# One store per 128 output rows in chunks 0 to 6 of an attention and feed-forward kernel

## The chip, the cores and the metric

The kernel runs on one core of a Trainium2 chip. The metric is the device time of one execution in microseconds (us). Before the change the median of three runs is 240.99 us (240.96 to 241.0). One execution was recorded by the hardware profiler; it took 240.52 us, of which the profile's span covers 238.4 us.

## What is computed

Eight batches of linear attention (8 heads, 576 tokens, 64 columns per head) are followed by a feed-forward block over all 4608 tokens. All inputs and the output are float32; the kernel computes its products in 16-bit floats.

```python
q_s = np.exp(q - np.max(q, axis=-1, keepdims=True))
q_s = q_s / (np.sum(q_s, axis=-1, keepdims=True) + 1e-09)
k_s = np.exp(k - np.max(k, axis=2, keepdims=True))
k_s = k_s / (np.sum(k_s, axis=2, keepdims=True) + 1e-09)
kv = np.einsum('bhsd,bhse->bhde', k_s, v)
y = np.einsum('bhsd,bhde->bhse', q_s, kv)
# feed-forward over x = y as [4608, 512]
a = x @ w1 ; b = x @ w2           # [4608, 1024] each
h = (a * b) @ w3                  # [4608, 1024]
out = h @ w_out                   # [4608, 512]
```

The softmax of q runs along the 64 columns, that of k along the tokens (axis 2). The kernel folds w3 and w_out into one matrix W3O of 1024 x 512 once, so that each token goes through w1, w2 and W3O only.

## The kernel before

**Tiling.** The 576 tokens of a batch are seen as 64 groups of 9 (`"(p j) c"`, p = 64, j = 9). A chunk is a set of 512 tokens: chunks 0 to 7 take tokens j = 0 to 7 of one batch each, chunk 8 takes the tokens j = 8 of all eight batches. Each chunk runs through `up` (matmuls with w2, then w1, line 779), `bs` (a cast of the w2 product from PSUM), `ab` (their product, line 794), and then four `down` steps of 128 tokens each (line 801), each with an eviction `os` (line 806, through the helper `copy` of line 323) into a buffer `osb` of 128 partitions x 512 float32, and a store `st` (line 824). A row block tb of chunk c covers j = 2 tb in partitions 0 to 63 and j = 2 tb + 1 in partitions 64 to 127. `osb` has four buffers, used in the order of the evictions; an eviction into a buffer waits until the store of what it held has landed.

**Order.** `ORDER` (line 77) lists every step by name, and each engine executes its own steps in that order: `st.4.2` is the store of row block 2 of chunk 4, `down.6.0` the down product of row block 0 of chunk 6, `xm.7.0` a product of attention that makes the x tile of chunk 7, and so on. A step that waits holds up everything behind it on its engine.

**SP.** SP (SyncE) issues four sorts of transfers in this order: the two loads of q for batch 0 (512 and 640 KB); the seventeen `LATE` loads of q, k and v for batches 2 to 7 (1152 KB each; line 402); twelve transposing transfers `qd` (line 637) that turn the normalised exponentials of q (tile `en`) into `qT` for batches 2 to 7, which `xm` needs; and the stores. In chunks 0 to 7 a store step issues two transfers of 64 rows each (line 827), in chunk 8 one transfer per row block of 128 rows, the last block in two halves of the columns (line 809). That makes 2 + 17 + 12 + 64 + 5 = 100 transfers on SP. They signal eight semaphores in turn, the first transfer the first one.

**End.** After its last transfer SP waits at the end of the program (line 915) for all eight semaphores, one after the other, and then meets the other engines at a barrier.

**The last part of attention.** The last two transposing transfers are `qd.7.0` and `qd.7.1`. On SP the stores `st.4.1`, `st.4.0` and `st.3.3` stand before the former, `st.5.1` and `st.4.2` between the two, and `st.4.3`, `st.5.2` and `st.5.0` behind the latter. With those of the earlier chunks, 20 row blocks of stores stand ahead of `qd.7.1`, and 8 of chunks 4 to 6 behind it. `xm.7.0`, `xm.7.1` and `xt.7` on TensorE wait for `qd.7.1`, and all of chunk 7 waits for them.

Of the kernel before, what the change touches and what calls it, by code (L numbers as in the profile page):

```python
# [229 lines left out]
def kernel(  # L230
# [11 lines left out]
    nc = tc.nc  # L242
    B, H, S, D = q.shape
# [7 lines left out]
    HALF = P // G  # L251
    HH = H // G
    NHP = HH // 2
    NJ = S // HALF
# [33 lines left out]
    st = {}  # L288
# [24 lines left out]
    TREE = [b < TREES for b in range(B)]  # L313
    VCAST = [b < VCASTS for b in range(B)]
    DMATP = []
    XMS = 3
    DMAT = [[b > DMATS or (b, p) in DMATP for p in range(2)] for b in range(B)]
    SPLIT = [0, 1]
# [153 lines left out]
    def attention(b):  # L472
# [176 lines left out]
        def XRING(name):  # L649
            if name[1] < XMS:  # L650
                return "att"
            return "pab" if name[0] == "xt" else "po" if name[2] else "att"
# [112 lines left out]
    def chunk(c):  # L765
# [54 lines left out]
        def os2(tb, c0, c1, eng):  # L820
            st["osb", c, tb, c0] = work.tile([P, c1 - c0], F32, tag="osb", name="osb", bufs=4)
            copy(eng, st["osb", c, tb, c0], st["po", c, tb, c0][:, 0:c1 - c0])

        def store(tb):
            for i in range(2):
                b, j = c, 2 * tb + i
                nc.sync.dma_start(
                    out=out[b * S:(b + 1) * S, :].rearrange("(p j) c -> p j c", j=NJ)[:, j, :],
                    in_=st["osb", c, tb][i * HALF:(i + 1) * HALF, :])

        A = plan.add
        nf = len(SUBS[c])
# [19 lines left out]
        for sub in range(nf):  # L852
            for tb in range(4):
                if not SUBS[c][sub][0] <= tb * P < SUBS[c][sub][1]:
                    continue
                first = tb * P == SUBS[c][sub][0]
                needs = (([("ab", c, sub, u) for u in range(nu - 1)] + [("W3O", ft) for ft in range(N_FT)]
                          if first else []) + ([("down", c, tb - 1)] if tb else []))
                late = [("ab", c, sub, nu - 1)] if first else []
                if c < B:  # L860
                    A(("down", c, tb), "PE", 1.75, lambda tb=tb: down(tb), needs, takes="po", after=late)
                    A(("os", c, tb), moves(C), 0, lambda eng, tb=tb: os(tb, eng), [("down", c, tb)],
                      lead=EVICT, gives=[("down", c, tb)], takes="osb")
                    A(("st", c, tb), "SP", 1.15, lambda tb=tb: store(tb), [("os", c, tb)], lead=1e3,
                      gives=[("os", c, tb)], size=P * C * 4)
                    continue
                cuts = [0, C // 2, C] if tb == 3 else [0, C]
                for c0, c1 in zip(cuts, cuts[1:]):
                    it = (c, tb, c0) if c1 < C else (c, tb)
                    A(("down", *it), "PE", 0.02 + 1.73 * (c1 - c0) / C,  # L870
                      lambda tb=tb, c0=c0, c1=c1: down2(tb, c0, c1), needs, takes="po", after=late)
                    A(("os", *it), moves(c1 - c0), 0,
                      lambda eng, tb=tb, c0=c0, c1=c1: os2(tb, c0, c1, eng), [("down", *it)],
                      lead=EVICT, gives=[("down", *it)], takes="osb")
                    A(("st", *it), "SP", 0.57, lambda tb=tb, c0=c0, c1=c1: tail(tb, c0, c1),
                      [("os", *it)], lead=1e3, gives=[("os", *it)], size=P * (c1 - c0) * 4)
                    needs, late = needs + [("down", *it)], []
# [42 lines left out]
```

## Time and profile before

| | |
|---|---|
| median of three runs | 240.99 us (240.96 to 241.0) |
| the profiled execution, its own time | 240.52 us |
| its span in the profile | 238.4 us |
| bytes written to HBM | 9.44 MB, all of it the output |
| bytes read from HBM | 38.80 MB |
| stores of chunks 0 to 7 | 64 transfers of 128 KB |
| stores of chunk 8 | 3 transfers of 256 KB, 2 of 128 KB |

The page of the profile gives each engine's busy time; the span cut into 40 equal slices with the busy share of each engine and of the 16 DMA engines; the DMA queues; the chain of work that ended last, followed back from the end; and the costliest groups of instructions. Times are in us from the start of the span. PE is TensorE's matmul, PEld its weight load, DVE is VectorE, ACT ScalarE, POOL GpSimd, SP SyncE; SPq is SP's own queue, which issues transfers. A DMA packet is one contiguous piece that one DMA engine moves. "q1 hardware_dynamic" are the transfers that SP issued; "q0 software_dynamic" those that GpSimd issued, all in the first 58 us. The share of a queue is the time that its packets took, as a share of 16 engines over the stretch asked for; packets overlap a little, so it can pass 100%.

### The profile page before, as it was taken

How to read it: one execution, taken by the hardware profiler on the slowest of the kernel's cores; microseconds unless marked ns; L12 is line 12 of the kernel's file. 1: busy time of each engine (PE TensorE's matmuls, PEld its weight loads, DVE VectorE, ACT ScalarE, POOL GpSimd, SP SyncE). 2: the span in 40 equal slices, each digit the busy share in tenths (PEclk: the TensorE clock that was granted, in tenths of full speed). 3: DMA queues.
4: the chain of work that ended last, by engine and by line, in shares of the span. 5: the costliest groups of instructions: out<-in, count | busy, mean ns of one | idle time of the engine just before them, and what ended most of it. 6: DMA issues, size and time to landing. Idle time of an engine off the chain costs nothing.

```text
span 238.4 us, 4957 instructions
## 1 busy us (share of the span) xinstructions
PE 230.7 (97%) x1981; PEld 121.1 (51%) x1981; DVE 180.0 (76%) x275; ACT 120.7 (51%) x221; POOL 112.8 (47%) x74
## 2 busy tenths in 40 slices
PE   7899899999999999999999999999999999999994
PEld 2445559865857544444444444444454444444442
DVE  2977998898899989998998899787567444355610
ACT  1436764668768958768824683557323002200021
POOL 8345445479957986997662933328530000000000
PEclk9999999999999999999999999999999999999999
DMA  6999999999989999688988932540077231030143
GB/s 209 215 294 223 322 220 301 261 370 392 389 210 291 403 205 294 243 235 203 327 270 200 306 147 46 77 111 0 0 150 173 62 71 45 0 91 0 44 132 132
DMA packets 37894, 45.66 MB, mean 192 GB/s; under 512 B 15984, under 2 KB 22384, under 8 KB 37872
## 3 DMA queue, kind: packets, MB, share of 16 engines
q1 hardware_dynamic: 30080, 34.22, 49.3%
q0 software_dynamic: 7792, 11.14, 21.3%
q8 instruction: 15, 0.25, 0.4%
q14 instruction: 7, 0.06, 0.1%
HBM read 38.80 MB, written 9.44 MB: 202 GB/s over the span
## 4 chain that ended last, share of the span: by engine, by line
PE 86%; DMA 5%; DVE 3%; POOL 2%; issue 1%; ACT 1%; POOLq 0%; ACTq 0%
PE pab L779 52%; PE po L801 23%; DMA wosb<-in_moe_w_out_dram 5%; PE po L816 3%; PE pkv L544 2%; PE po L452 2%; PE xm L662 1%; DVE k L519 1%; POOL en L614 1%; POOL w L402 1%; PE po L662 1%; DVE kmx L493 1%; ACT ek L527 0%; PE pkv L554 0%; PE qtp L629 0%
## 5 line engine op out<-in xcount | busy, mean ns | idle before, releaser
L779 PE MATMUL pab<-x,w2sb 128*128 128x512 f16 (+1 forms) x320 | 66.0, 337 | 0.1
L779 PE MATMUL pab<-x,w1sb 128*128 128x512 f16 (+1 forms) x320 | 65.9, 336 | 0.0
L794 DVE TENSOR_TENSOR ab<-pab,bsb 128x512 f16<-128x512 f32 x72 | 48.9, 681 | 16.7 <-PE pab L779 15.2
L801 PE MATMUL po<-W3O,ab 128*128 128x512 f16 x256 | 59.5, 379 | 0.0
L779 PEld LDWEIGHTS <-w1sb 128*128 128x128 f16 x352 | 34.4, 98 | 27.9
L779 PEld LDWEIGHTS <-w2sb 128*128 128x128 f16 x352 | 33.4, 98 | 27.0 <-issue 0.7
L323 ACT CAST bsb<-pab 128x512 f16<-128x512 f32 x49 | 28.3, 585 | 36.5 <-PE pab L779 36.2
L801 PEld LDWEIGHTS <-ab 128*128 128x128 f16 x256 | 24.6, 98 | 28.8 <-issue 0.4
L519 POOL TENSOR_TENSOR k<-k,cb 128x1152 f32<-128x1152 f32 x13 | 33.9, 2626 | 8.1 <-DVE km L496 3.5
L582 POOL TENSOR_TENSOR q<-q,qm 128x1280 f32<-128x1280 f32 (+1 forms) x13 | 27.8, 2142 | 20.7 <-DVE qm L577 12.9
L614 POOL TENSOR_TENSOR en<-eq,qr 128x1024 f16<-128x1024 f16 (+1 forms) x14 | 29.2, 2093 | 17.4 <-DVE qr L607 8.0
L323 ACT COPY osb<-po 128x512 f32<-128x512 f32 (+1 forms) x26 | 14.9, 576 | 35.8 <-PE po L801 28.9
L577 DVE TENSOR_REDUCE qm<-q 128x16 f32<-128x1024 f32 (+1 forms) x16 | 21.4, 1340 | 3.5 <-DMA q<-in_q_dram 3.5
L323 DVE COPY osb<-po 128x512 f32<-128x512 f32 (+1 forms) x11 | 7.3, 667 | 20.8 <-PE po L801 13.7
L595 DVE TENSOR_REDUCE qr<-eq 128x16 f32<-128x1024 f16 (+1 forms) x16 | 21.3, 1341 | 0.5 <-ACT eq L590 0.5
L590 ACT ACTIVATE eq<-q 128x1024 f16<-128x1024 f32 (+1 forms) x16 | 18.6, 1163 | 5.6 <-DVE q L582 3.0
L527 ACT ACTIVATE ek<-k 128x1152 f16<-128x1152 f32 x16 | 18.6, 1165 | 3.6 <-POOL k L519 2.4
L323 DVE CAST bsb<-pab 128x512 f16<-128x512 f32 x23 | 15.8, 687 | 2.7 <-PE pab L779 2.2
L484 DVE TENSOR_REDUCE km<-k 128x128 f32<-128x1152 f32 x8 | 16.9, 2138 | 0.0
L452 PE MATMUL po<-wosb,w3T 128*128 128x512 f16 x64 | 15.0, 379 | 0.6 <-DMA wosb<-in_moe_w_out_dram 0.5
L327 ACT ACTIVATE x<-xm 128x512 f16<-128x512 f32 x14 | 7.9, 596 | 5.5 <-PE xm L662 5.4
L350 PE MATMUL po<-zero 128*128 128x512 f16 x25 | 8.4, 509 | 1.6 <-DVE zero L345 1.6
(70 smaller groups left out, 197.9 us busy)
## 6 DMA issues: line engine op xcount, KB each, us to landing
out_dram<-osb SPq DMA_DIRECT2D x66, 128.0 KB, 2.4
q<-in_q_dram SPq DMA_DIRECT2D x6, 1152.0 KB, 6.8
v<-in_v_dram SPq DMA_DIRECT2D x6, 1152.0 KB, 8.5
k<-in_k_dram SPq DMA_DIRECT2D x5, 1152.0 KB, 7.0
k<-in_k_dram POOLq DMA_DIRECT2D x3, 1152.0 KB, 14.6
v<-in_v_dram POOLq DMA_DIRECT2D x2, 576.0 KB, 14.4
w<-in_moe_w_dram POOLq DMA_DIRECT2D x2, 512.0 KB, 12.0
w<-in_moe_w_dram POOLq DMA_DIRECT2D x4, 256.0 KB, 14.0
```

The lines of the kernel that those rows point to most:

```text
L323: return [(nc.scalar.copy if eng == "ACT" else engine[eng].tensor_copy)(out=out, in_=in_)]
L452: nc.tensor.matmul(st["pf", ft], lhsT=st["w3T", ft][:, gt, :], rhs=wosb[:, gt, :], start=(gt == 0), stop=(gt == N_FT - 1))
L519: return [engine[eng].tensor_tensor(out=kb[:, two(hp), :, :], in0=kb[:, two(hp), :, :], in1=st["cb", b][:, two(hp), None, :].broadcast_to( ...
L527: nc.scalar.activation(out=st["ek", b][:, hp, :, :].rearrange("p j (i d) -> p i j d", i=2), in_=kb[:, two(hp), :, :], func=AF.Exp)
L577: dve.tensor_reduce(out=st["qm", b][:, :, j], in_=qb[:, :, j, :], axis=AX.X, op=ALU.max)
L582: return [engine[eng].tensor_tensor(out=qb[:, :, j, :], in0=qb[:, :, j, :], in1=st["qm", b][:, :, j, None].broadcast_to([P, HH, n, D]), op ...
L590: nc.scalar.activation(out=st["eq", b, p], in_=qb[:, :, j, :], func=AF.Exp)
L595: dve.tensor_reduce(out=st["qr", b][:, :, slice(*PARTS[p])], in_=st["eq", b, p], axis=AX.X, op=ALU.add)
L614: return [engine[eng].tensor_tensor(out=st["en", b][:, j, :, :].rearrange("p j h d -> p h j d"), in0=st["eq", b, p], in1=st["qr", b][:, :, ...
L779: nc.tensor.matmul(st["p", one, c, sub, u][:, a * (t1 - t0):(a + 1) * (t1 - t0)], lhsT=w[:, ct, fb * P:(fb + 1) * P], rhs=x()[:, ct, t0:t1 ...
L794: dve.tensor_tensor(out=st["ab", c][:, nf * u:nf * u + nf, t0:t1], in0=cut(st["p", 0, c, sub, u]), in1=cut(st["bsb", c, sub, u]), op=ALU.mult)
L801: nc.tensor.matmul(st["po", c, tb], lhsT=st["ab", c][:, ft, tb * P:(tb + 1) * P], rhs=W3O[:, ft, :], start=(ft == 0), stop=(ft == N_FT - 1))
```

## The change

A row block of chunks 0 to 6 is stored by one transfer of 128 rows in place of two of 64. The output side of that transfer is a view with three dimensions, [2, 64, 512]: two values of j, 64 groups p, 512 columns; the buffer's side is [128 partitions, 512]. In chunk 7 two transfers per row block remain, and their output side is [1, 64, 512]. Chunk 8 is as it was. SP then issues 2 + 17 + 12 + 28 + 8 + 5 = 72 transfers, and the 72nd, being a multiple of eight, signals the last of the eight semaphores; the 100th of before signalled the fourth.

```diff
     DMATP = []
+    APART = [7]
     XMS = 3
...
         def store(tb):
-            for i in range(2):
-                b, j = c, 2 * tb + i
-                nc.sync.dma_start(
-                    out=out[b * S:(b + 1) * S, :].rearrange("(p j) c -> p j c", j=NJ)[:, j, :],
-                    in_=st["osb", c, tb][i * HALF:(i + 1) * HALF, :])
+            to = out[c * S:(c + 1) * S, :].rearrange("(p j) c -> j p c", j=NJ)
+            n = 1 if c in APART else 2
+            for i in range(2 * tb, 2 * tb + 2, n):
+                r = (i - 2 * tb) * HALF
+                nc.sync.dma_start(out=to[i:i + n], in_=st["osb", c, tb][r:r + n * HALF, :])
```

## The prediction

> **What bounds the kernel now.** I read the page first: the busy times, the DMA slices and the chain that ended last.
>
> ```profile
> span 238.4 us, 4957 instructions
> ...
> PE 230.7 (97%) x1981; PEld 121.1 (51%) x1981; DVE 180.0 (76%) x275; ACT 120.7 (51%) x221; POOL 112.8 (47%) x74
> ...
> DMA  6999999999989999688988932540077231030143
> ...
> PE 86%; DMA 5%; DVE 3%; POOL 2%; issue 1%; ACT 1%; POOLq 0%; ACTq 0%
> ```
>
> PE is busy for 97% of the span and makes 86% of the chain. The DMA engines are nearly full for the first 60% of it (digits of 9 and 8 up to the 23rd slice) and have room later. So PE sets the time, and the transfers are hidden as long as they keep up. The chain in order of time shows where the last transfer that PE needs comes in, and what is left then.
>
> ```profile
> 176.46 6.04 PE pab L779 x28
> 182.50 0.34 PE xm L662 x4
> 182.84 0.22 PE po L662 x4
> ...
> 228.12 6.94 PE po L816 x40
> 235.06 0.03 ACTq L323
> 235.08 0.04 issue
> 235.12 0.37 ACT osb L323
> ```
>
> From 182.50, where chunk 7's x is made (`xm.7`), PE has work without a gap up to 235.06. What holds up PE there is added to the end in full, up to what the end takes back. SP's queue around that place, in order of time:
>
> ```profile
> 153.23 3.70 SPq L827 DMA_DIRECT2D out_dram<-osb  x6
> 172.36 2.08 SPq L637 DMA_TRANSPOSE qT<-en  x1
> 174.54 2.46 SPq L827 DMA_DIRECT2D out_dram<-osb  x4
> 177.10 1.39 SPq L637 DMA_TRANSPOSE qT<-en  x1
> 178.58 51.29 SPq L827 DMA_DIRECT2D out_dram<-osb  x24
> ```
>
> The transfer at 177.10 is `qd.7.1`; `xm.7` waits for it, and the stores of 20 row blocks stand ahead of it on SP.
>
> **What a store costs the DMA engines.** Two stretches of the DMA view hold nothing but stores: 232.30 to 234.24 one store of 128 rows (chunk 8), 221.70 to 224.00 the two of 64 rows of one row block. A third row is the stretch from 67 to 178.
>
> ```profile
> DMA packets 144, 0.26 MB, mean 135 GB/s; under 512 B 16, under 2 KB 16, under 8 KB 144
> ...
> q1 hardware_dynamic: 144, 0.26, 35.9%
> ```
> ```profile
> DMA packets 160, 0.26 MB, mean 114 GB/s; under 512 B 32, under 2 KB 32, under 8 KB 160
> ...
> q1 hardware_dynamic: 160, 0.26, 49.1%
> ```
> ```profile
> q1 hardware_dynamic: 21809, 21.30, 68.7%
> ...
> out_dram<-osb SPq DMA_DIRECT2D x38, 128.0 KB, 4.9
> q<-in_q_dram SPq DMA_DIRECT2D x4, 1152.0 KB, 6.3
> v<-in_v_dram SPq DMA_DIRECT2D x4, 1152.0 KB, 7.9
> k<-in_k_dram SPq DMA_DIRECT2D x3, 1152.0 KB, 6.3
> qT<-en SPq DMA_TRANSPOSE x12, 3.4
> ```
>
> Each transfer has 16 small packets, its signals, one from each of 16 engines; the rest are rows of 2 KB. The 128-row store takes 0.359 x 16 x 1.94 = 11.1 engine-us for 128 rows, 87 ns a row; the pair 0.491 x 16 x 2.30 = 18.1, or 141 ns a row. On each engine that is 8 x 87 ns = 0.70 us for a whole block and 8 x 141 ns = 1.13 us for a block in two halves. So rows are not dealt to engines at random: 64 rows, which lie in one half of the partitions, are dearer on 16 engines than 128 that lie in both.
>
> **Removed and moved.** 28 SP issues go, and the remaining ones start earlier.
>
> ```profile
> L827 SPq DMA_DIRECT2D out_dram<-osb x64: 466/587/1522, 58.9 to 229.3; - x64
> ...
> DMA to landing us min/median/max: 2.2/2.4/10.1
> ```
> ```profile
> L809 SPq DMA_DIRECT2D out_dram<-osb x5: 332/332/382, 230.5 to 235.5; - x5
> ...
> DMA to landing us min/median/max: 1.7/2.0/2.1
> ```
>
> That is 28 x 0.59 = 16 us of SP. SP's work is behind PE's, and PE has no gap in the chain to give back, so I cost it at nothing. If that cover were gone, each store step would free what stands behind it by one issue, 0.59 us, no more.
>
> **The end.** The waits on the eight semaphores stand in order; in the stretch 237.20 to 237.53 the profile shows
>
> ```profile
> L915 SPq EVENT_SEMAPHORE  x5: 28/28/28, 237.2 to 237.5; - x5
> ```
>
> The first of the five follows the last landing (the fourth semaphore); four more follow it, in 0.2 to 0.4 us by the rounded starts: about 0.06 each, 0.25 together. With 72 transfers the last landing is the eighth semaphore's and these four lie before it. That is a gain of 0.25 us.
>
> **Added: how many engines share the new transfer.** Before, both sides of every store have an outer count of 64 or 128, and 16 engines take 4 or 8 rows each. The new output side has an outer count of 2, the buffer's side 128. No transfer in the trace has an outer count below 64 on a side, so I bound the price. Cheapest: 16 engines take 8 rows each, as in chunk 8, 0.70 us on each engine, less than the 1.13 of now. Dearest: the outer count is what is dealt out, the two sides have only 2 in common, and two engines take 64 rows each: 64 x 87 ns = 5.57 us on both, at the other fourteen nothing. (At the 141 ns of the half stores it would be 9.0; but there 16 engines work on one half of the partitions at a time, here one on each, so I take 87.) Between them lie 4 engines, 2.8 us, and 8, 1.4 us.
>
> I take two engines. For it speak that in all rows above the work is shared by the outer count, evenly, with one signal from each engine, and that the price of a row depends on which rows go together. Against it, that the trace can't show what a count of 2 does.
>
> [...]
>
> **The sum.** An engine's queue takes SP's transfers in their order, so engines 0 and 1 (call them so) have everything behind a store wait for it. From 67 to 178 an engine is busy 0.687 x 111 = 76.3 us. In that are 11 loads, 12 transposing transfers and 20 row blocks of stores (38 issues, and the two of 58.9, the first of which land some 10 us later). The blocks cost 20 x 1.13 = 22.6 us now and 20 x 5.57 = 111.4 us after. So the two engines need 76.3 - 22.6 + 111.4 = 165.1 us for the same list, and are at 67 + 165.1 = 232.1 where they now are at 178: 54.1 us later. The 34.7 us of room that an engine has in that stretch are used up in this. `qd.7.1` lands 3.4 us after its issue, at 180.5, and PE takes it up at 182.50: 2.0 us are in hand, and 52.1 us reach PE.
>
> Do the two engines ever run dry? SP holds each transposing transfer for 1.4 to 2.1 us (rows above), and stores wait for PE, which is late by then too; each such hole adds. The steps of PE are pushed back in small parts, from `xm.3` on, each time by less than the queue; I add nothing, and put 0 to 15 us into the range.
>
> Behind `qd.7.1` a second stall follows. `os.6.0` takes the buffer of `os.5.0`, whose store is the third behind `qd.7.1`.
>
> ```profile
> 188.44 0.69 DVE L323 COPY osb<-po 128x512 f32<-128x512 f32 x1 [2.62 <-PE po L801]
> 189.30 0.69 DVE L323 CAST bsb<-pab 128x512 f16<-128x512 f32 x1 [0.17 <-PE pab L779]
> ```
> ```profile
> 191.69 1.89 PE L801 MATMUL po<-W3O,ab 128*128 128x512 f16 x8
> 193.42 1.03 PE L779 MATMUL pab<-x,w2sb 128*128 128x512 f16 x4
> ```
>
> The store is done at 180.5 + 54.1 + 3 x 5.57 = 251.3; `os.6.0` would start at 188.44 + 52.1 = 240.5 and waits 10.8 us on DVE, with the cast `bs.7.0.0` behind it. PE goes on until it needs the accumulator that this cast frees, at 193.42 + 52.1 = 245.5, and gets it after copy and cast, at 251.3 + 2 x 0.69 = 252.7: 7.2 us. What is left (five blocks of chunks 5 and 6 and the half stores of chunk 7) drains during the 42 us that PE still works, so that the end keeps its length but for the 0.25.
>
> Sum: 52.1 + 7.2 - 0.25 = 59 us. The profiled execution took 240.52, which is 0.47 below the median of the runs; 240.52 + 59 = 299.6, and I forecast **300 us**. Its own range comes from the price of a row and the holes.
>
> ```profile
> GB/s 209 215 294 223 322 220 301 261 370 392 389 210 291 403 205 294 243 235 203 327 270 200 306 147 46 77 111 0 0 150 173 62 71 45 0 91 0 44 132 132
> ...
> 0.00:50.00 50.00, 45.76 (x440) 28.80 (x441) 40.35 (x67) 25.41 (x44) 25.90 (x33) 1.00 1.12 258
> ```
>
> The fullest slice moves 403 GB/s, 25.2 per engine, which is 81 ns for 2 KB; packets overlap by up to 12% (share 1.12), so 72 ns is the least: 20 x 64 x 15 ns = 19 us less, and without the second stall 274. A row a tenth dearer (11 us) and holes of 15 us give 326. At 141 ns a row it would be 369, which I hold for unlikely (0.05).
>
> **The rivals.**
> *Sixteen engines after all.* The output's 128 rows are shared as in chunk 8. For it: chunk 8's rows, 87 ns. Against: there both sides count 128. Then only the end changes: 240.99 - 0.25 = 240.7. This is the other side, and the count of engines decides it: with 8 rows per engine the queue at 178 is 20 x 0.43 = 9 us shorter, and nothing waits.
> *The freed SP time counts.* As before, and stores land sooner, so that loads start up to 0.59 us earlier. Against: no wait for a DMA stands in the chain after the start, where a DMA makes 5%. Time 240.3 at best.
> *Four or eight engines.* Eight cost 20 x (1.4 - 1.13) = 5 us in a stretch with 34.7 us of room: 240.7 to 241.5. Four cost 33 us, just that room, with waits where the room isn't: 245 to 255. Nothing in the rows speaks for either.
>
> **How the numbers follow.** Two engines 0.77; sixteen 0.17; freed time 0.03; four or eight 0.03. The first and two thirds of the last are slower by over 0.2%, which is about what a measurement of this kernel can tell from no change: 0.79. Sixteen, at -0.1%, and the rest are within it: 0.18. Faster: 0.03. The time is that of the likeliest case. The range must take in the sixteen engines to leave out no more than 2 in 10; from 240.4 to 318 it leaves out the upper tail of the two engines and the best of the freed time, about 0.12; the likeliest case alone has 274 to 326.
>
> **What would show it.** Right: a new row store lands some 7 us after issue where nothing is ahead (1 us to start, 5.6 for the rows), the DMA view shows an eighth of the engines busy while it runs, the transposing transfers land tens of us later, PE has long gaps before `xm` (line 662) and waits for them, the last wait at line 915 is followed by no other semaphore's. Wrong: a landing of about 2 us and a share like chunk 8's, or the same delay without idle on PE. The size is wrong if a row on two engines takes another time than 87 ns, or if the two queues run dry.

## The result and the profile after

The changed kernel takes 289.02 us (median of 5 runs, 287.39 to 289.38) where the kernel before takes 241.0 us in the same comparison (240.96 to 241.27): a ratio of 1.197, 95% interval 1.194 to 1.201. It is 48 us slower. The profiled execution took 287.39 us, its span is 285.6 us, 47.2 more than before.

First the page of the changed kernel: span, busy times, the slices (PEclk is the granted clock of PE in tenths of full speed, DMA the busy share of the engines) and the chain that ended last.

```profile
span 285.6 us, 4917 instructions
...
PE 239.7 (84%) x1981; PEld 123.8 (43%) x1981; DVE 180.8 (63%) x275; ACT 121.1 (42%) x221; POOL 113.0 (40%) x74
...
PEclk9999999999999856997579999986999779999999
DMA  7999999998931946999669721941129211112234
...
q1 hardware_dynamic: 29240, 34.21, 51.6%
...
PE 62%; DMA 22%; issue 4%; POOL 3%; ACT 3%; DVE 3%; POOLq 1%; SPq 1%; DVEq 0%; ACTq 0%
```

PE's share of the span falls from 97% to 84%, and DMA's share of the chain rises from 5% to 22%. The DMA row has many digits of 1: one tenth or a little more of the 16 engines. PE executes the same 1981 matmuls but is busy 9 us longer, and the clock row shows 5 to 8 behind the gaps. SP's packets fall from 30080 to 29240. That is 840 = 28 x 30: each of the 28 joint stores replaces two transfers with 16 signals each by one with 2.

Next a stretch of the changed kernel in which the DMA engines move almost nothing but joint stores (the new transfers of 128 rows), 229 to 249; two packets are of other queues.

```profile
DMA packets 510, 1.05 MB, mean 52 GB/s; under 512 B 8, under 2 KB 8, under 8 KB 508
...
q1 hardware_dynamic: 508, 1.02, 13.1%
```

508 packets of SP, of which 8 are small (the signals): 500 rows in 20 us. The share is 13.1%, two engines of sixteen (12.5%) busy without a break. Each moves 250 rows in 20 us, so a row takes 80 ns and a joint store 64 x 80 ns = 5.1 us.

Who waits is in PE's waits, and where is in the chain in order of time (start, length, what). First the changed kernel:

```profile
PE xm L663 <- DMA qT<-en: 22.3, 3, 9.8
PE po L663 <- DMA qT<-en: 14.3, 1, 14.3
```
```profile
102.64 5.05 DMA qT<-en
...
107.82 0.64 PE po L663 x4
...
127.84 12.30 DMA qT<-en
...
140.28 0.64 PE xm L663 x3
...
162.09 0.41 PE po L663 x4
...
192.74 0.64 PE xm L663 x4
...
216.74 11.61 DMA qT<-en
...
228.40 0.64 PE xm L663 x4
```

The same rows of the kernel before:

```profile
91.72 0.34 PE po L662 x4
...
112.25 0.34 PE xm L662 x4
...
131.08 0.34 PE po L662 x4
...
155.06 0.34 PE xm L662 x4
...
182.50 0.34 PE xm L662 x4
```

PE waits four times for `qT`, the output of the transposing transfers, 36.6 us in all: for batches 3, 4, 6 and 7. The x products of batches 3 to 7 start 16.1, 28.0, 31.0, 37.7 and 45.9 us later than before. So most of the time arises step by step between 75 and 228.

Busy time by stretch closes the sum; the columns are the stretch, its length, the busy time of PE, PEld, DVE, ACT and POOL with their instructions, the granted clock, the DMA share and GB/s. Changed kernel, then the kernel before with the matching stretches:

```profile
0.00:70.60 70.60, 65.79 (x765) 41.91 (x765) 58.74 (x93) 41.83 (x71) 42.69 (x41) 1.00 1.09 281
70.60:228.40 157.80, 119.81 (x962) 56.84 (x962) 98.19 (x148) 69.24 (x131) 70.29 (x33) 0.88 0.69 137
228.40:282.60 54.20, 54.12 (x264) 25.05 (x263) 23.86 (x35) 9.64 (x19) 0.00 (x0) 0.97 0.22 70
282.60:285.60 3.00, 0.00 (x0) 0.00 (x0) 0.00 (x0) 0.37 (x1) 0.00 (x0) 1.00 0.38 130
```
```profile
0.00:70.20 70.20, 65.96 (x763) 42.02 (x765) 58.78 (x93) 41.80 (x71) 42.67 (x41) 1.00 1.09 286
70.20:182.50 112.30, 112.21 (x965) 54.58 (x968) 96.89 (x147) 68.92 (x131) 70.11 (x33) 1.00 0.70 195
182.50:235.10 52.60, 52.54 (x264) 24.50 (x264) 24.35 (x36) 9.62 (x18) 0.00 (x0) 1.00 0.25 63
235.10:238.40 3.30, 0.00 (x0) 0.00 (x0) 0.00 (x0) 0.37 (x1) 0.00 (x0) 1.00 0.36 122
```

Up to `xm.7` the kernel loses 0.4 + 45.5 us, behind it 1.6, and it gains 0.3 at the end: 47.2. In the long stretch PE is also busy 7.6 us longer (119.81 against 112.21), at a granted clock of 0.88; the rest of the 45.5 is idle time. The average DMA share of the long stretch is the same as before (0.69 and 0.70): a mean over sixteen engines doesn't show that two of them are full.

### The profile page after: what moved, and what is told of

The parts are those of the page before. It is cut to its first block, busy times and chain, and to the rows that moved or that the text cites. A ratio compares the mean times of both kernels' runs of the same rounds, so it can differ in the third digit from the quotient of the medians.

```text
span 285.6 us, 4917 instructions
## 1 busy us (share of the span) xinstructions
PE 239.7 (84%) x1981; PEld 123.8 (43%) x1981; DVE 180.8 (63%) x275; ACT 121.1 (42%) x221; POOL 113.0 (40%) x74
## 4 chain that ended last, share of the span: by engine, by line
PE 62%; DMA 22%; issue 4%; POOL 3%; ACT 3%; DVE 3%; POOLq 1%; SPq 1%; DVEq 0%; ACTq 0%
PE pab L780 38%; PE po L802 16%; DMA qT<-en 12%; DMA w<-in_moe_w_dram 6%; DMA out_dram<-osb 4%; PE po L817 2%; PE pkv L545 2%; PE xm L663 1%; PE po L453 1%; POOL q L583 1%; DVE k L520 1%; POOLq L916 1%; PE po L663 1%; ACT ek L528 1%; ACT v L324 1%
## 5 line engine op out<-in xcount | busy, mean ns | idle before, releaser
L780 PE MATMUL pab<-x,w2sb 128*128 128x512 f16 (+1 forms) x320 | 70.3, 352 | 0.1
L780 PE MATMUL pab<-x,w1sb 128*128 128x512 f16 (+1 forms) x320 | 68.6, 346 | 0.0
L780 PEld LDWEIGHTS <-w1sb 128*128 128x128 f16 x352 | 35.1, 100 | 30.5 <-issue 4.6
L780 PEld LDWEIGHTS <-w2sb 128*128 128x128 f16 x352 | 34.2, 100 | 29.6 <-issue 5.2
L663 PE MATMUL xm<-qT,kv 64*64 64x256 f16 (+1 forms) x60 | 5.5, 394 | 22.4 <-DMA qT<-en 22.3
L663 PEld LDWEIGHTS <-kv 64*64 64x64 f16 x144 | 4.4, 126 | 44.0 <-issue 28.2
L330 DVE TENSOR_SCALAR x<-po 128x512 f16<-128x512 f32 x4 | 2.8, 689 | 21.9 <-PE po L663 21.9
```

Of the source, the lines that this page charges most:

```text
L780: nc.tensor.matmul(st["p", one, c, sub, u][:, a * (t1 - t0):(a + 1) * (t1 - t0)], lhsT=w[:, ct, fb * P:(fb + 1) * P], rhs=x()[:, ct, t0:t1 ...
```

## The experiments

The theory after this: the outer count of 2 on the output side puts a joint store on two engines (5.1 us on each), and it costs time where transfers that PE waits for stand behind it in SP's order. Seven kernels tell this from its rivals. All ratios are against the kernel before in the same comparison.

**Place: the same four joint stores, late (e1) or early (e2).** Only the list of chunks that keep two transfers differs.

```diff
-    APART = [7]
+    APART = [0, 1, 2, 3, 4, 5, 7]   # e1: joint in chunk 6 alone
+    APART = [1, 2, 3, 4, 5, 6, 7]   # e2: joint in chunk 0 alone
```

> Joint stores of 128 rows in chunk 6 alone (four of them, 96 transfers on SP, so that the last signals the eighth semaphore). Theory (two engines move such a store at about 5.1 us each, and what costs time is that transfers PE waits for stand behind it in SP's order): nothing that PE needs stands behind the stores of chunk 6, so no stall; the end is shorter by 0.25 us: 240.75. Rival (each joint store costs its share of the 48 us wherever it stands, 28 of them): 4 x 48 / 28 = 6.9 us more, 247.9.

> The same edit in chunk 0 alone, again four joint stores and 96 transfers. Theory: the four stores stand ahead of the transposing transfers of batches 2 and 3, which PE takes up within 2 to 3 us of their landing now; three of the stores in a row delay those of batch 3 by about 3 x 4 = 12 us and waits for osb buffers come on top, so 250 to 256. Rival (a fixed share each): 247.9, as for chunk 6.

Chunk 6 alone: 240.5 us, ratio 0.998 (0.997 to 0.999). Chunk 0 alone: 253.69 us, ratio 1.052 (1.051 to 1.054). Both have four joint stores and 96 transfers, so there is no fixed price of a joint store. The joint stores of chunk 6 are slow too: a stretch with little else (191 to 197.6) shows two small packets and two engines' share (first rows below, chunk 6 alone), and by the trace's signals three of the four land 7.7 to 7.8 us after issue, the fourth, queued behind two others, 10.3. No transfer that PE waits for stands behind them. With chunk 0 the stall is at `xm.3`, in one wait (last row, PE's waits):

```profile
DMA packets 140, 0.28 MB, mean 43 GB/s; under 512 B 2, under 2 KB 2, under 8 KB 140
...
q1 hardware_dynamic: 140, 0.28, 12.9%
```
```profile
PE po L663 <- DMA qT<-en: 9.8, 1, 9.8
```

The x product there starts at 103.39, 11.7 us later than before; what comes behind it takes some 2 us longer, and its first matmuls are slow again (1.89 us for four). The waits for `osb` that were expected on top are there as well, 12.0 us on ACT, but most of that passes beside the stall.

**Outer count against two token columns (e4).** The second rival said that a joint store is slow by its addresses: two columns of tokens, 9 rows apart within a group and interleaved in memory. In this kernel, in chunks 2 to 6, the product of w1 and w2 is written so that the two tokens of a group lie in neighbouring partitions of `osb`. The store then moves the same 128 rows to the same addresses, with an output side of [64, 2, 512]. Chunks 0, 1 and 7 keep two transfers per row block. Parts of the edit, against the changed kernel:

```diff
-    APART = [7]
+    APART = [0, 1, 7, 8]
...
+            to = st["ab", c][:, nf * u:nf * u + nf, t0:t1]
+            if c not in APART:
+                cut = lambda t: t.rearrange("p (b k c) -> p b k c", k=2, c=HALF)
+                to = st["ab", c][:, u, :].rearrange("p (b c k) -> p b k c", k=2, c=HALF)
...
+                nc.sync.dma_start(out=to[:, 2 * tb:2 * tb + 2, :], in_=st["osb", c, tb][:, :])
```

> Chunks 2 to 6 stored with one transfer of 128 rows per row block, as in the change, but with the product of the feed-forward written so that the two tokens of a group lie in neighbouring partitions: the output side is then [64, 2, 512] and counts 64 outermost. 80 transfers on SP, the last on the eighth semaphore. Theory: sixteen signals and sixteen engines, landing about 2 us after issue as in chunk 8, no stall: 240.75, unless the strided writes of the product cost VectorE time. Rival (a joint store of two token columns is slow by its addresses, not by its outer count): most of the 48 us again, above 270.

240.47 us, ratio 0.997 (0.996 to 0.998); no wait of PE for `qT` is left. A stretch with one of these stores alone (190.4 to 192.3) has sixteen signals and is done within it:

```profile
DMA packets 144, 0.26 MB, mean 138 GB/s; under 512 B 16, under 2 KB 16, under 8 KB 144
...
q1 hardware_dynamic: 144, 0.26, 36.6%
```

The rival falls: same rows, same addresses, other outer count, no loss. The strided write costs VectorE little: the product's instructions take 707 ns on average over all 72, 681 before.

**Is it the divisor, or the two columns (e5)?** Here each half store of chunk 6 of the kernel before is cut in two, with one token column in each, and with row counts whose largest divisors up to 16 are 2, 15, 14 and 1.

```diff
+    CUT = {(6, 0): 62, (6, 1): 60, (6, 2): 56, (6, 3): 61}
...
+                cuts = [0, CUT.get((c, tb), HALF), HALF]
+                for r0, r1 in zip(cuts, cuts[1:]):
+                    if r0 < r1:
+                        nc.sync.dma_start(
+                            out=out[b * S:(b + 1) * S, :].rearrange("(p j) c -> p j c", j=NJ)[r0:r1, j, :],
+                            in_=st["osb", c, tb][i * HALF + r0:i * HALF + r1, :])
```

> The kernel before, with each half store of chunk 6 cut into two transfers of one token column: 62 + 2 rows in row block 0, 60 + 4 in block 1, 56 + 8 in block 2, 61 + 3 in block 3. Theory (the largest number up to 16 that divides the outer counts of both sides is the number of engines; a store of 64 rows per engine lands 7.75 us after issue, of which 64 x 0.080 = 5.1 are rows, so 2.6 are fixed): 62 rows run on two engines, 31 rows each, and land 5.1 us after issue; 61 rows run on one engine and land at 7.5; 60 and 56 rows run on fifteen and fourteen engines, 4 rows each, and land at 2.2 to 2.4, as 64 rows do. Rival (what is slow is the output side of two token columns, and a single column goes over sixteen engines whatever its count): all of them land at 2.2 to 2.4. The time: 241.0 by both; 108 transfers end on the fourth semaphore, as before.

One execution: 240.77 us beside 240.98 for the kernel before. From issue to the last signal in the trace: the first 62 rows 5.25 us, the first 61 rows 7.38 us, 56 rows 1.82 us. The 60 rows took 3.06 us behind a 62-row transfer that was still on the way. The signals at the end of the data number 2 for 62 rows, 15 for 60, 14 for 56 and 1 for 61 (one more update of the semaphore comes 0.4 to 0.5 us after issue). 62 rows on one column are slow and 56 are not, so it is the divisors of the count, not the two columns. In all four the number of signals is the largest number up to 16 that divides the row count; the joint store, with outer counts of 2 and 128, has two. The landings agree with this as the number of engines for 61, 62 and 56; for 60 they can't tell.

**The end alone (e3).** The kernel before with four transfers more, so that 104 end on the eighth semaphore; every store still counts a multiple of 16 rows (32, 64 or 128).

```diff
+    QUARTERS = [(6, 0), (6, 1)]
...
+            m = HALF // 2 if (c, tb) in QUARTERS else HALF
+            for r in range(0, P, m):
+                b, j, r0 = c, 2 * tb + r // HALF, r % HALF
...
```

> The kernel before with the first two row blocks of chunk 6 stored in quarters of 32 rows instead of halves of 64: 104 transfers on SP, the last of which signals the eighth semaphore; all transfers on sixteen engines. Theory: four waits of 0.06 us move ahead of the last landing, 240.99 - 0.25 = 240.75. Rival (the order of the semaphores doesn't matter): 241.0.

240.55 us, ratio 0.998 (0.997 to 0.999). The gain is real, 0.5 us by the medians, at least 0.3 by the interval, somewhat more than the 0.25 that the four waits explain. The kernels with 80 and with 96 transfers gained as much. Their common trait is a multiple of eight; what the rest of the half microsecond is was not settled.

**How far the sum carries: chunks 4 to 6 (e6).**

```diff
-    APART = [7]
+    APART = [0, 1, 2, 3, 7]
```

> Joint stores in chunks 4, 5 and 6 (88 transfers on SP). Theory: four of the twelve stand ahead of the last transposing transfer, and two of these, st.5.1 and st.4.2, directly ahead of it, issued at 174.5 and 175.1 to 175.8: two stores of 5.13 us from about 176, then the transposing transfer's 1.3, so that it lands at about 188 in place of 180.5; PE wants it at 182.5 and stalls 5 to 6 us there and nowhere else. With the 0.25 of the end 246.0 (245 to 247). Rival (a fixed share for each joint store, 12 x 1.7): 261. Rival (only the number of bytes on two engines counts, and these have room here): 240.75.

249.3 us, ratio 1.036 (1.034 to 1.039), 3 us more than expected. There is one stall, at `xm.7`, as the theory says, and both rivals fall. Two sizes were off. The wait is 6.7 us. And behind it PE is slow (PE in order of time, then the stretch behind the stall by windows):

```profile
189.57 0.64 PE L663 MATMUL xm<-qT,kv 64*64 64x512 f16 x4 [6.75 <-DMA qT<-en]
...
190.68 1.89 PE L780 MATMUL pab<-x,w2sb 128*128 128x512 f16 x4
192.36 1.48 PE L780 MATMUL pab<-x,w1sb 128*128 128x512 f16 x4
193.67 3.62 PE L802 MATMUL po<-W3O,ab 128*128 128x512 f16 x16
```
```profile
189.60:193.70 4.10, 4.10 (x25) 1.75 (x25) 1.98 (x3) 1.43 (x4) 0.00 (x0) 0.55 0.14 55
```

The same work of the kernel before:

```profile
182.45:184.80 2.35, 2.35 (x26) 1.17 (x26) 2.26 (x4) 1.42 (x4) 0.00 (x0) 1.00 0.48 112
```

4.1 us in place of 2.35 at a granted clock of 0.55. 6.7 and 1.7, less the gain of the end, make about 8.1 of the 8.3 measured.

**Is it the idling that slows the clock (e7)?** The kernel of chunks 4 to 6 with PE kept busy during that wait by 28 matmuls of zeros.

```diff
-    "begin": 17, "pf.5.0": 8,
+    "begin": 17, "pf.5.0": 8, "xm.7.0": 28,
```

> The kernel of e6 (joint stores in chunks 4, 5 and 6; 249.3 us) with 28 matmuls of zeros on TensorE in front of xm.7, where PE waited 6.7 us for the last transposing transfer; at 0.22 us each they fill about 6.1 us of that wait. Theory: the stretch right behind the wait took 4.1 us at a granted clock of 0.55 where the kernel before takes 2.35 at 1.00, because PE had been idle; with PE busy it takes 2.4 again, and the time is 249.3 - 1.7 = 247.6. Rival (the stretch is long for another reason, such as operands that come late): 249.3.

247.36 us, ratio 1.029 (1.025 to 1.032), 1.9 us less than without the matmuls of zeros. The runs lie between 246.8 and 248.67, but the intervals of the two ratios don't overlap. PE in order of time:

```profile
183.04 6.21 PE L351 MATMUL po<-zero 128*128 128x512 f16 x28
189.18 0.41 PE L663 MATMUL xm<-qT,kv 64*64 64x512 f16 x4
...
189.80 1.04 PE L780 MATMUL pab<-x,w2sb 128*128 128x512 f16 x4
190.67 1.03 PE L780 MATMUL pab<-x,w1sb 128*128 128x512 f16 x4
```

The four matmuls with w2 behind the stall take 1.04 us again, in place of 1.89. The profiled spans differ by 2.1 us (247.0 and 244.9): `xm.7` starts 0.4 earlier here (189.18 and 189.57), and the other 1.7 is what the clock had cost. Over the whole span the granted clock is 0.999 here and 0.986 in e6. How long PE must idle for this, or stay busy to undo it, no run tests.

## Why the prediction was right, and where its sizes were off

**The bound.** PE sets the time as long as the transfers keep up: right. `xm.7` was the right place to read the loss from; 45.9 of the 47.2 us have arisen there.

**Two engines.** Right, though an estimate: no row of the kernel before shows what a count of 2 does. The page's packet count and the 13.1% share show it, and e4 and e5 that the outer count is the cause.

**The price of a row.** 87 ns was taken from a store that sixteen engines share; on two engines it is 80. Over 64 x 20 rows on each engine that is 9 us too much, the largest error of the sum.

**The queue up to `qd.7.1`.** With 5.13 us for a store (from one landing to the next by the trace's signals, 238.43 to 243.56) the prediction's own sum gives 76.3 - 22.6 + 102.6 = 156.3 us, 45.3 later than before, less the 2.0 in hand: 43.3. Measured 45.9, 2.6 more. The sum let the two engines never run dry, and they did. The DMA view of the changed kernel from 209 to 214.5 holds no store's row, and nothing at all before 213 (40 slices, busy tenths; what comes then is a packet of another queue and a transposing transfer):

```profile
DMA  0000000000000000000000000000007006999999
```

SP stood at `qd.7.0` there, which waited for the normalised exponentials from POOL; these were late because PE's stall at `xm.6` had held up VectorE and ScalarE ahead of them. So one unbroken queue up to `qd.7.1`, as in the sum, is not what happened: 37.7 us were lost by `xm.6` and passed on through the engines, and 8.2 came after that, with the two joint stores directly ahead of `qd.7.1` (216.74 to its landing, 11.61 us, in the chain above, where 3.4 were forecast). The 0 to 15 us that the range held for holes covered the gap. It lasts over 4 us, more than the 2.6, so another term of the sum must be too large, and that the two nearly cancel is luck. Which term was not traced; one that may be is the first of the 20 blocks, which the sum counts in full although it was issued at 59.3, ahead of the 67 from which it counts.

**The second stall behind `qd.7.1`, 7.2 us.** This step failed: there was none. `os.6.0` waited for PE alone (VectorE in order of time, changed kernel):

```profile
235.91 0.69 DVE L324 COPY osb<-po 128x512 f32<-128x512 f32 x1 [2.76 <-PE po L802]
```

The prediction gave it the buffer of `os.5.0`, in the order of the evictions. The traces show another order. In e6 `os.5.2` waits for a store and starts at 183.13 (ScalarE in order of time):

```profile
183.13 0.58 ACT L324 COPY osb<-po 128x512 f32<-128x512 f32 x1 [7.46 <-DMA out_dram<-osb]
```

By the trace's signals `st.5.1` lands at 182.99 in that run and `st.4.2` at 188.12. By the order of evictions it would have had to wait for `st.4.2`; it took the buffer of the store that stands first on SP, `st.5.1`. So buffers are passed on in the order of the stores in `ORDER`, as far as these places show, and the sentence on them in the description of the kernel above is wrong. By that order `os.6.0` had the buffer of `os.4.3`, whose store is the first behind `qd.7.1` and landed at 233.3, in time. It can't have had that of `os.5.0`: `st.5.0` landed at 243.56 only, 7.6 us after `os.6.0` had started.

**The clock.** The sum had no term for it. Behind the last stall PE needs 1.5 us more than the 2.35 us of before (changed kernel, by windows); e7 shows for the same place, behind a wait of 6.7 us, that idling is the cause.

```profile
228.40:232.25 3.85, 3.85 (x24) 1.67 (x24) 1.98 (x3) 1.43 (x4) 0.00 (x0) 0.58 0.15 56
```

The earlier stalls have their slow matmuls too. From `xm.4` to `xm.5` PE took 21.8 us in place of 18.8, without a wait for `qT`; the wait at `xm.6` takes this up again, as the queue sets the time there. Behind `xm.6` nothing does: the chain that ended last runs through PE's slow matmuls (changed kernel, then the same 32 before) to the exponentials that `qd.7.0` and `qd.7.1` wait for, so that about 1.8 us of the 45.9 come from the clock.

```profile
193.91 8.79 PE pab L780 x32
...
210.43 1.91 POOL en L615
```
```profile
155.68 7.01 PE pab L779 x32
```

**The end.** 0.25 forecast, about 0.3 seen in the profile. It does not decide anything beside 48 us, but e3 shows that it is there.

Put together: 52.1 + 7.2 - 0.25 was forecast, 45.9 + 1.6 - 0.3 measured. Two of the errors (row price, buffer) made the forecast 16 us too high; what the queue took beyond its sum and the clock behind `xm.7` made it 4 us too low.

**The rivals.** Sixteen engines, with 0.17, is what e4 built in chunks 2 to 6, and its forecast time of 240.7 is near e4's 240.47. Freed time on SP gave nothing that could be told from the end's gain: e4 issues 20 transfers fewer than the kernel before and stands within 0.1 us of e3, which issues four more.

## What to carry to other kernels

Before joining transfers, look at the outermost count of both sides and what divides both: a leading dimension of 2 put all 256 KB of a store on two engines here (share 13.1%), 62 rows gave two signals and 60 gave fifteen (e5), and a mean DMA share didn't show it (0.69, and 0.70 before). Count the signals (small packets) per transfer in the profile; in these runs they tell the number of engines (16 signals at a share of 36.6% in e4, 2 at 12.9% in e1). A slow transfer cost nothing by itself in e1 (ratio 0.998); price it by what stands behind it in the same queue, and add the slow clock of TensorE behind a stall (1.5 to 1.8 us behind those of 6 to 7 us here).

The gain that the change has at its end can be had without its loss: 104, 96 or 80 transfers, as in e3, e1 and e4, are 0.2% to 0.3% faster than the kernel before.

## What the runs showed of the hardware that was not expected

SP itself took longer to issue while a few joint stores were under way. In the changed kernel the three stores that SP issues from 74.13 on take 15.15 us to issue and the load behind them 4.93, where the issue of a store there takes 0.59 us at the median (36 issues, the longest 9.17; SP's queue in order of time):

```profile
73.56 0.45 SPq L403 DMA_DIRECT2D v<-in_v_dram  x1
74.13 15.15 SPq L830 DMA_DIRECT2D out_dram<-osb  x3
89.38 4.93 SPq L403 DMA_DIRECT2D q<-in_q_dram  x1
94.41 11.19 SPq L638 DMA_TRANSPOSE qT<-en  x2
```

What SP waits for in them, no run tests. And a row of 2 KB takes 80 ns on two engines that have the machine for themselves, 87 when sixteen move 128 rows, 141 when sixteen move 64.
